# Windowed attention in 64-key blocks on small array tiles, with one score phase and one exp per unit

## The chip, the cores and the metric

The kernel runs on one core of a Trainium2 chip. The core has a matrix engine (PE, whose weight loads are shown apart as PEld), a vector engine (DVE), an activation engine (ACT), a general engine (POOL) and a queue engine for transfers (SP), which run side by side and wait for one another through semaphores. The metric is the time of the kernel on the device in microseconds (us), lower being better.

## The reference

Two branches share a layer norm `xn` of the input (2048 tokens, 512 features, bf16). The attention branch computes, with 32 heads of 16 features,

```python
off = jnp.arange(8) * 2                       # the token itself and 7 more, two apart
idx = pos[:, None] - off[None, :];  mask = idx >= 0
logits = einsum("bhsd,bhswd->bhsw", q, k[idx]) * 16 ** -0.5     # -1e9 where not mask
s = (einsum("bhsw,bhswd->bhsd", softmax(logits), v[idx])) @ wo
```

The other branch is a mixer with an MLP: `x1 = xn + shifted(gelu(LN(xn) @ w1)) @ w2`, then `x1 + gelu(LN(x1) @ w3) @ w4` with 1376 hidden features. The output is `x + s * silu(other branch)`.

Because the offsets are two apart, a token only meets tokens of its own parity: in each parity's own order, of 1024 tokens, a query attends to itself and the 7 tokens ahead of it.

## The kernel before

The tokens are held by parity (p = 0, 1). The first half of the kernel makes the projections: transposed q and k (lines 317 to 323), the shifted mixer (329 to 362), the first MLP matmul w3 (392 to 399). The transposed k and q are kept twice (e = 0, 1 for even and odd heads), so that a group of 32 partitions holds 16 features of one head and 16 rows of a mask; the mask rows come from a table in DRAM through `fill_mask` (lines 218 to 227), and their product pushes a score outside of the window far below zero. So a score matmul has 32 rows, and exp needs no mask of its own. The mask rows repeat with a period of 15 groups of 8 tokens, that is 120.

Attention then runs in **units** (lines 52 to 57): a unit has up to 128 keys of one parity and the 120 queries whose windows lie in them; the first unit has 128 queries with 128 keys, the last 56 with 64. With 9 units for each parity there are 18, taken in order by the loop at line 652. In each iteration n:

- `scores(p, u, 0)`: 16 matmuls of 32 rows by 128 columns (line 461), four row tiles of the array at a time, into two PSUM tiles `s` and `t` of two banks each; for each of them one exp on ACT (line 468) of 128 x 960, which writes the unnormalised weights `prob`.
- first fill: part of a `w4` tile (line 413, 11 matmuls a tile; the second MLP matmul; line 420 to 423 then apply its residual and the silu by DVE, ACT, DVE), scalings, an output tile.
- `scores(p, u, 1)`: the other 16 matmuls and two exps, into the same PSUM tiles.
- second fill: the rest of the `w4` tile.
- `weighted` of the unit before (line 489): 32 matmuls of 128 rows by 32 columns, four column tiles at a time; the stationary operand is `v_aug`, 16 columns of values and 16 of the constant 2, so that each head also yields its denominator. One DVE cast (line 496) gathers the result in `orw`.
- `values` of the next unit (line 440): 4 dense matmuls, and a DVE cast to `v_aug` (line 445).
- last fill: loads and stores.

All these matmuls are pinned (`pin`): they run in the order written. The other instructions are ordered by a planner.

Each parity's units form three **runs** (line 61: units 0 to 2, 3 to 5, 6 to 8), with two `orw` buffers in all. At the end of a run `normalise` sends the denominators through DRAM to a dense layout (SP, lines 511 and 517) and the numerators to `oT` by eight POOL DMAs (line 521). Two units later `normalise_mid` takes the reciprocals on DVE (line 533) and spreads them by SP DMAs (534, 539); four units later `normalise_end` scales `oT` (line 545). Then `final_tile` (line 573) can multiply 128 tokens by `wo`, and DVE and POOL or DVE finish them (582, 584).

Eight PSUM banks are shared out at line 616: two for `s`, two for `t`, two for `o`, one for `w` (w4 tiles), one for `b` (values and `wo`). Tiles 0 to 7 of `w4` go to units 0 to 7, tiles 8 to 11 to the rest; parity 0's eight output tiles go to units 10 to 17. Behind the loop (lines 666 to 686, the **tail**) come w4 tiles 12 to 15, the last scalings and parity 1's eight output tiles.

## Time and profile before

| | us |
|---|---|
| times of three runs | 224.55, 227.35, 228.18 (median 227.35) |
| span of the profiled execution | 222.8 (its time is not given beside it) |
| first stage to the first complete score phase | 0 to 114.1 |
| attention loop, 18 units | 114.1 to 199.3 |
| tail | 199.3 to 222.8 |
| DVE casts of the weighted sum, line 496 | 19.7 for 18 |
| exp on ACT, line 468 | 62.7 for 72 |

A span is counted from the first to the last instruction of the program; the time has some start and end around it. "PE busy" counts the modelled length of pipelined matmuls, so it says that PE has work and not that it is at its peak. Small matmuls on different tiles of the array overlap; what such a phase costs is read from the starts of the phases, not from the sum of the instructions. In a view by stage, the granted clock of PE is given as a share of full speed: it is 0.70 between 114.08 and 119.71, and 1.00 in the rest of the loop.

### The profile page before, as it was taken

To read this page: it belongs to the slowest core of one execution; us is meant where nothing else is said; L and a number is where in the kernel's file an instruction comes from. 1 tells how busy PE (TensorE), PEld (TensorE's weight loads), DVE (VectorE), ACT (ScalarE), POOL (GpSimd) and SP (SyncE) were. 2 spreads that over 40 slices of the span, in tenths; PEclk is the share of its full clock that TensorE was granted. 3 is DMA by queue.
4 is the path that set the end of the run, shared out by engine and by line. 5 is a ranking of instruction groups with operands and counts; after the bars stand their busy time and mean duration, and the time that the engine had idled before them with its cause. 6 is when DMAs were issued, how large, how long until landed. Compare 5 with 4: busy or idle time off the path is not lost.

```text
span 222.8 us, 4851 instructions
## 1 busy us (share of the span) xinstructions
PE 205.6 (92%) x1992; PEld 95.3 (43%) x1992; DVE 130.1 (58%) x244; ACT 136.2 (61%) x158; POOL 61.9 (28%) x119
## 2 busy tenths in 40 slices
PE   8799999999999999999869999999969999999961
PEld 2335545444444444444323444444434445454420
DVE  6689964127279683000103566678457857795984
ACT  2086696956913615665457888898776978842110
POOL 1723563502002202000000007015074482947040
PEclk9999999999999999999988999999999999999998
DMA  5999100130390675799995005526650342625222
GB/s 160 371 392 388 47 0 4 4 8 0 122 161 3 171 195 154 170 118 121 119 122 60 0 3 119 157 68 159 209 125 13 101 83 70 154 51 148 67 85 94
DMA packets 32957, 25.60 MB, mean 115 GB/s; under 512 B 16152, under 2 KB 28792, under 8 KB 32936
## 3 DMA queue, kind: packets, MB, share of 16 engines
q1 hardware_dynamic: 30312, 22.16, 42.7%
q0 software_dynamic: 1536, 2.10, 4.9%
q10 hardware_dynamic: 1088, 1.05, 1.3%
q8 instruction: 15, 0.25, 0.5%
q14 instruction: 6, 0.05, 0.1%
HBM read 16.58 MB, written 4.52 MB: 95 GB/s over the span
## 4 chain that ended last, share of the span: by engine, by line
PE 67%; DMA 10%; DVE 8%; ACT 7%; POOL 2%; SPq 2%; issue 2%; DVEq 0%; ACTq 0%
PE w_ps L413 17%; PE qk_ps L317 9%; PE w_ps L392 9%; ACT prob L468 6%; PE w_ps L329 6%; PE w_ps L357 6%; PE s_ps L461 5%; PE v_ps L440 5%; PE wo_ps L573 4%; DMA qT_159<-mask_d 4%; DMA kT_155<-mask_d 4%; PE o_ps L489 3%; DVE l1s L253 2%; SPq L224 2%; DMA oT_1494<-orw 2%
## 5 line engine op out<-in xcount | busy, mean ns | idle before, releaser
L468 ACT ACTIVATE prob<-s_ps 128x960 bf16<-128x960 f32 (+2 forms) x72 | 62.7, 925 | 15.1 <-PE s_ps L461 14.1
L413 PE MATMUL w_ps<-w_sb,h3T 128*128 128x512 bf16 (+1 forms) x176 | 44.9, 390 | 0.0
L392 PE MATMUL w_ps<-x1nT,w_sb 128*128 128x512 bf16 (+1 forms) x176 | 38.3, 379 | 0.0
L397 ACT ACTIVATE h3T<-w_ps 128x1024 bf16<-128x1024 f32 x20 | 20.5, 1024 | 25.6 <-PE w_ps L392 23.3
L521 POOL DMA_DIRECT2D oT_1494<-orw x24 | 12.4, 523 | 68.2 <-DVE orw L496 68.2
L392 PEld LDWEIGHTS <-w_sb 128*128 128x128 bf16 (+1 forms) x176 | 17.6, 100 | 20.4
L413 PEld LDWEIGHTS <-h3T 128*128 128x128 bf16 (+1 forms) x176 | 15.1, 99 | 17.3 <-issue 1.0
L496 DVE CAST orw<-o_ps 128x960 bf16<-128x960 f32 (+2 forms) x18 | 19.7, 1098 | 1.3 <-PE o_ps L489 1.1
L445 DVE CAST v_aug_148<-v_ps 128x512 bf16<-128x512 f32 (+1 forms) x9 | 6.1, 682 | 23.0 <-PE v_ps L440 23.0
L317 PEld LDWEIGHTS <-wqk_sb 128*128 128x128 bf16 x128 | 12.1, 98 | 12.9
L317 PE MATMUL qk_ps<-xnT_152,wqk_sb 128*128 128x512 bf16 x64 | 15.3, 379 | 0.8 <-DVE xnT_152 L291 0.8
L420 DVE TENSOR_TENSOR xn_95<-w_ps,xn_95 128x512 bf16<-128x512 f32 x8 | 5.5, 684 | 16.5 <-PE w_ps L413 16.5
L329 PE MATMUL w_ps<-xn2T,w_sb 128*128 128x512 bf16 x64 | 14.6, 379 | 0.0
L317 PE MATMUL qk_ps<-xnT_153,wqk_sb 128*128 128x512 bf16 x64 | 14.5, 379 | 0.0
L584 POOL TENSOR_TENSOR xo_1715<-sg,xo_1715 128x512 bf16<-128x512 bf16 x8 | 10.4, 1297 | 14.5 <-DVE sg L582 13.4
L362 DVE TENSOR_TENSOR xn_95<-w_ps,xn_95 128x1024 bf16<-128x1024 f32 x4 | 4.9, 1215 | 14.4 <-PE w_ps L357 14.4
L422 ACT ACTIVATE sig<-xn_96 128x512 bf16<-128x512 bf16 x8 | 5.0, 630 | 12.6 <-DVE xn_96 L420 12.6
L521 POOL DMA_DIRECT2D oT_2418<-orw x24 | 12.1, 513 | 1.6 <-DVE orw L496 1.6
L246 POOL TENSOR_SCALAR l3r<-l3m 128x4 f32<-128x4 f32 x4 | 0.9, 232 | 36.7 <-DVE l3m L254 36.7
L440 PE MATMUL v_ps<-wv_sb,xnT_153 128*128 128x512 bf16 (+1 forms) x36 | 9.3, 380 | 2.0 <-DVE sg L582 2.0
L461 PE MATMUL s_ps<-qT_159,kT_155 32*128 32x120 bf16 (+2 forms) x144 | 7.7, 214 | 3.1 <-DMA qT_159<-mask_d 3.1
L573 PE MATMUL wo_ps<-wo_sb,oT_2418 128*128 128x512 bf16 x32 | 7.6, 379 | 2.2 <-DVE oT_2418 L545 2.2
(132 smaller groups left out, 329.3 us busy)
## 6 DMA issues: line engine op xcount, KB each, us to landing
w_sb<-in_B_w_dram SPq DMA_DIRECT2D x1, 1376.0 KB, 9.5
w_sb<-in_B_w_dram SPq DMA_DIRECT2D x1, 1280.0 KB
wqk_sb<-in_A_wqkv_dram SPq DMA_DIRECT2D x2, 512.0 KB
w_sb<-in_B_w_dram SPq DMA_DIRECT2D x2, 512.0 KB, 6.0
xn_96<-in_A_x_dram SPq DMA_DIRECT2D x4, 256.0 KB, 6.9
xo_1715<-in_A_x_dram SPq DMA_DIRECT2D x4, 256.0 KB, 5.5
xo_2325<-in_A_x_dram SPq DMA_DIRECT2D x4, 256.0 KB, 4.5
out_dram<-xo_1715 SPq DMA_DIRECT2D x4, 256.0 KB, 3.8
```

The costliest lines, as they stand in the source:

```text
L317: nc.tensor.matmul(pt[:, b, :], lhsT=wqk_sb[:, dt, nt * P : (nt + 1) * P], rhs=xnT[p][:, dt, cs], start=(dt == 0), stop=(dt == ND - 1),)
L329: nc.tensor.matmul(pt[:, b, :], lhsT=w1_sb[:, dt, g * P : (g + 1) * P], rhs=xn2T[:, dt, :], start=(dt == 0), stop=(dt == ND - 1),)
L357: nc.tensor.matmul(pt[:, j, :], lhsT=w2_src(p, g, m0), rhs=w2_sb[:, g, :], start=(g == 0), stop=(g == ND - 1),)
L392: nc.tensor.matmul(pt[:fs, ft % 2, :], lhsT=w3_sb[:, dt, ft * P : ft * P + fs], rhs=x1nT[:, dt, :], start=(dt == 0), stop=(dt == ND - 1),)
L397: last["gelu"] = nc.scalar.activation(h3T[:, 2 * a : 2 * a + 2, :], pt, AF.Gelu_apprx_tanh)
L413: nc.tensor.matmul(pt, lhsT=h3[c][:fs, ft, jj * P : (jj + 1) * P], rhs=w4_sb[:fs, ft, :], start=(ft == 0), stop=(ft == NF - 1),)
L440: nc.tensor.matmul(vp[:nk, :], lhsT=xnT[p][:, dt, k0 : k0 + nk], rhs=wv_sb[:, dt, :], start=(dt == 0), stop=(dt == ND - 1),)
L461: nc.tensor.matmul(st[:nk, b, i * nq : (i + 1) * nq], lhsT=kT[p][e][r : r + 32, dt, k0 : k0 + nk], rhs=qT[p][e][r : r + 32, dt, q0 : q0 + ...
L468: nc.scalar.activation(prv[:nk, 2 * h : 2 * h + 2], st[:nk, :, 0 : 4 * nq], AF.Exp, scale=SCALE)
L496: nc.vector.tensor_copy(out=orw[p][:, :, :, q0 - ra : q0 - ra + nq], in_=op[:, :, 0 : 4 * nq].rearrange("p j (s q) -> p j s q", q=nq),)
L521: nc.gpsimd.dma_start(out=oT[p][DH * hh : DH * (hh + 1), :, ra : ra + rw], in_=orw[p][32 * cg : 32 * cg + DH, jj],)
L573: nc.tensor.matmul(pt[:, j, :], lhsT=oT[p][:, dt, (i + j) * P : (i + j + 1) * P], rhs=wo["sb"][:, dt, :], start=(dt == 0), stop=(dt == ND ...
```

## The change

Keys are taken in blocks of 64 in place of 128. A unit has still 128 keys, two blocks s = 0, 1 on the lower and upper half of the partitions, and block s meets 64 queries alone: keys k0 to k0+63 meet queries k0+8 to k0+71, keys k0+64 to k0+127 meet queries k0+64 to k0+127. The 8 queries k0+64 to k0+71 are met by both blocks, and their two partial sums, numerators and denominators, are added. So a unit yields 120 queries again, and units start at k0 = 56 + 120 u, eight for each parity. The first 64 tokens of both parities, with the first 64 keys each, form one joint unit (`None`), in the loop between the parities: 17 units.

- `scores` is one phase: 64 matmuls of 32 rows by 64 columns with 64 queries each, on tiles at (32 r, 64 s), into one PSUM tile `s` of four banks, and one exp of 128 x 2048.
- `weighted` has 64 matmuls of 64 rows by 32 columns, on tiles at (64 s, 32 cg), with 64 queries each. DVE casts the 2 x 56 queries that only one block meets, copies the 8 shared ones of the second block to a small tile, and adds those of the first.
- In an iteration all fill work comes last: scores, weighted of the unit before, values of the next one, then the w4 part, scalings, output tile, loads and stores.
- Runs are units 0 to 2, 3 to 5, 6 to 7, and the joint unit is a run `first` of its own for both parities (16 POOL DMAs, two scalings), with its gathered result in a buffer of the `s4` group.
- Output tiles 1 to 7 of parity 0 go to units 10 to 16; tile 0 goes to the tail, and so does `normalise_mid` of parity 1's second run. The tail uses the four banks of `s` singly (f, g, h, i).
- The mask table is read 8 columns further on, to fit the new start of the units.

Lines that are taken out of `values`, `scores` and `weighted` are left out here; they stand above.

```diff
@@ -45,24 +45,20 @@
     NCH = S // CH
     TPC = CH // P
     M = S // 2
-    NQ = 120
     PEN = 512.0
-
-
-    units = [(0, P, 0, P)]
-    while units[-1][0] + units[-1][1] < M:
-        q0 = units[-1][0] + units[-1][1]
-        nq = min(NQ, M - q0)
-        units.append((q0, nq, q0 - W, nq + W))
+    KB = P // 2
+    QU = P - W
+
+
+    units = [KB - W + u * QU for u in range((M - KB) // QU)]
     NU = len(units)
 
 
     runs = []
-    for cuts in ((0, 3, 6, NU), (0, 3, 6, NU)):
-        runs.append(
-            [(a, b, units[a][0], sum(units[u][1] for u in range(a, b))) for a, b in zip(cuts[:-1], cuts[1:])]
-        )
-    RW = max(r[3] for rs in runs for r in rs)
+    for a, b in ((0, 3), (3, 6), (6, NU)):
+        q0 = units[a] + W
+        runs.append((a, b, q0, units[b - 1] + P - q0))
+    RW = max(r[3] for r in runs)
...
         nc.vector.tensor_tensor(
-            out=tab[:, :, 0:P], in0=tab[:, :, 0:P], in1=ident.unsqueeze(1).to_broadcast([P, 3, P]), op=ALU.mult
+            out=tab, in0=tab, in1=ident.unsqueeze(1).to_broadcast([P, 3, P]), op=ALU.mult
         )
         g = small.tile([P, 4], F32, name="mg", tag="mg", bufs=1)
-        nc.vector.tensor_reduce(out=g[:, 0:3], in_=tab[:, :, 0:P], axis=mybir.AxisListType.X, op=ALU.add)
...
     def values(p, u):
         va = v_aug[cnt["v"] % NV]
         cnt["v"] += 1
         vp = pst("b", "v_ps")[:, 0, :]
         for dt in range(ND):
+            first, last_ = dt == 0, dt == ND - 1
+            if p is None:
+                for s in range(2):
                     pin(
                         nc.tensor.matmul(
+                            vp[KB * s : KB * s + KB, :], lhsT=xnT[s][:, dt, 0:KB], rhs=wv_sb[:, dt, :],
+                            start=first, stop=last_, tile_position=(0, KB * s),
                         )
                     )
+            else:
+                k0 = units[u]
+                pin(
+                    nc.tensor.matmul(
+                        vp, lhsT=xnT[p][:, dt, k0 : k0 + P], rhs=wv_sb[:, dt, :], start=first, stop=last_
+                    )
                 )
+        nc.vector.tensor_copy(out=va[:, :, 0:DH], in_=vp.rearrange("p (h d) -> p h d", d=DH))
+        return va
+
+    def scores(p, u):
+
+        pr = sm4.tile([P, 4, 2 * ND, KB], BF16, name="prob", tag="s4")
+        st = pst("s", "s_ps").rearrange("p r (i q) -> p r i q", q=KB)
+        for i in range(2 * ND):
+            dt, e = i // 2, i % 2
+            for s in range(2):
+                pp, k0 = (s, 0) if p is None else (p, units[u] + KB * s)
+                q0 = k0 if p is None or s else k0 + W
+                for r in range(4):
+                    rows = slice(32 * r, 32 * r + 32)
                     pin(
                         nc.tensor.matmul(
+                            st[KB * s : KB * s + KB, r, i, :], lhsT=kT[pp][e][rows, dt, k0 : k0 + KB],
+                            rhs=qT[pp][e][rows, dt, q0 : q0 + KB], start=True, stop=True,
+                            tile_position=(32 * r, KB * s),
                         )
                     )
+        with tc.issue_after(last["gelu"].ins):
+            nc.scalar.activation(pr, st, AF.Exp, scale=SCALE)
+        return pr
+
+    def weighted(p, u, va, pr):
+
+        if p is None:
+            key, rw = "first", P
+        else:
+            r = next(i for i, x in enumerate(runs) if u < x[1])
+            key, (a, b, ra, rw) = (p, r), runs[r]
+        if p is None or u == a:
+            if p is None:
+                t = sm4.tile([P, 2 * ND * rw], BF16, name="orw0", tag="s4")
+            else:
+                t = orwp.tile([P, 2 * ND * RW], BF16, name="orw", tag="orw")[:, 0 : 2 * ND * rw]
+            orw[p] = t.rearrange("p (g q) -> p g q", g=2 * ND)
+        op = pst("o", "o_ps")
+        for g in range(2 * ND):
+            jj, dt = g // ND, g % ND
+            for s in range(2):
+                for cg in range(4):
+                    h = 4 * jj + cg
+                    pin(
+                        nc.tensor.matmul(
+                            op[32 * cg : 32 * cg + 32, s, g * KB : (g + 1) * KB],
+                            lhsT=va[KB * s : KB * s + KB, dt * 8 + h, :],
+                            rhs=pr[KB * s : KB * s + KB, h // 2, 2 * dt + h % 2, :],
+                            start=True, stop=True, tile_position=(KB * s, 32 * cg),
+                        )
+                    )
+        ow = orw[p]
+        ov_ = op.rearrange("p s (g q) -> p s g q", q=KB)
+        if p is None:
+            nc.vector.tensor_copy(out=ow.rearrange("p g (s q) -> p s g q", s=2), in_=ov_)
+            normalise(key, rw, [(0, 0, KB), (1, 0, KB)])
+        else:
+            c, n = units[u] + W - ra, KB - W
+            wide = lambda t, off, step, width: bass.AP(
+                t.tensor, t.offset + off, [list(t.ap[0]), [step, 2], list(t.ap[-2]), [1, width]]
+            )
+            nc.vector.tensor_copy(out=wide(ow, c, KB, n), in_=wide(ov_, 0, CH + W, n))
+            mix = small.tile([P, 2 * ND, W], F32, name="mix", tag="mix")
+            nc.vector.tensor_copy(out=mix, in_=ov_[:, 1, :, 0:W])
+            nc.vector.tensor_tensor(out=ow[:, :, c + n : c + KB], in0=ov_[:, 0, :, n:KB], in1=mix, op=ALU.add)
+            if u == b - 1:
+                normalise(key, rw, [(p, ra, rw)])
...
+        c = 0
+        for p, q0, nq in parts:
+            for jj in range(2):
+                for cg in range(4):
+                    hh = 4 * jj + cg
+                    nc.gpsimd.dma_start(
+                        out=oT[p][DH * hh : DH * (hh + 1), :, q0 : q0 + nq],
+                        in_=w[32 * cg : 32 * cg + DH, ND * jj : ND * jj + ND, c : c + nq],
+                    )
+            c += nq
+        rrs[key] = (dn, rden_d, w, rw, parts)
+
+    def normalise_mid(key):
+        dn, rden_d, w, rw, parts = rrs[key]
         n = H * rw // P
         rb = small.tile([P, n], BF16, name="rb", tag="rb", bufs=1)
...
@@ -613,76 +633,72 @@
     stage_w3(2)
     stage_w3(3)
 
-    layout(s=2, t=2, o=2, w=1, b=1)
+    layout(s=4, o=2, w=1, b=1)
     NW = 12
     w4s = [w4_tile(t // TPC, t % TPC, t >= NW) for t in range(S // P)]
 
-    fill = {n: ([], [], []) for n in range(2 * NU)}
-
-    for n in range(2 * NU):
-        t, a, b, c = (
-            (n, 0, 9, NF) if n < 8
-            else ((8, 0, 3, 4), (8, 4, 9, NF), (9, 0, 4, 4), (9, 4, 8, 8), (9, 8, NF, NF), (10, 0, 4, 4),
-                  (10, 4, 8, 8), (10, 8, NF, NF), (11, 0, 5, 6), (11, 6, NF, NF))[n - 8]
-        )
-        fill[n][0].append(lambda t=t, a=a, b=b: w4s[t](a, b))
+
+    order = [(0, u) for u in range(NU)] + [(None, 0)] + [(1, u) for u in range(NU)]
+    NN = len(order)
+    fill = [[] for _ in range(NN)]
+    split = (
+        [(8, 0, 6)], [(8, 6, NF)], [(9, 0, 4)], [(9, 4, 8)], [(9, 8, NF)], [(10, 0, 4)], [(10, 4, 8)],
+        [(10, 8, NF), (11, 0, 3)], [(11, 3, NF)],
+    )
+    for n in range(NN):
+        for t, a, b in [(n, 0, NF)] if n < 8 else split[n - 8]:
+            fill[n].append(lambda t=t, a=a, b=b: w4s[t](a, b))
         if n >= 10:
-            fill[n][0].append(lambda i=n - 10: final_tile(0, i, 1, nc.gpsimd))
-        if n >= 12 and n % 2 == 0:
-            fill[n][2].append(lambda i=n - 12: store(nc.sync, 0, i))
-        if c > b:
-            fill[n][1].append(lambda t=t, b=b, c=c: w4s[t](b, c))
-
-    for p in range(2):
-        for r, (_, end, _, _) in enumerate(runs[p]):
-            n = p * NU + end
-            if n + 2 < 2 * NU:
-                fill[n + 2][0].insert(0, lambda p=p, r=r: normalise_mid(p, r))
-            if n + 4 < 2 * NU:
-                fill[n + 4][0].insert(0, lambda p=p, r=r: normalise_end(p, r))
+            fill[n].append(lambda i=n - 9: final_tile(0, i, 1, nc.gpsimd))
+        if n in (12, 14, 16):
+            fill[n].append(lambda i=n - 10: store(nc.sync, 0, i))
+
+    ends = [((0, 0), 3), ((0, 1), 6), ((0, 2), 8), ("first", 9), ((1, 0), 12), ((1, 1), 15)]
+    for key, n in ends:
+        if n + 2 < NN:
+            fill[n + 2].insert(0, lambda key=key: normalise_mid(key))
+        if n + 4 < NN:
+            fill[n + 4].insert(0, lambda key=key: normalise_end(key))
     for w in range(2):
-        fill[w][2].append(lambda w=w: fill_mask(1, w))
-    fill[8][2].append(load_wo)
+        fill[w].append(lambda w=w: fill_mask(1, w))
+    fill[9].append(load_wo)
     for k in range(4):
-        fill[5 + k][2].append(lambda k=k: load_xo(0, k))
-        fill[11 + k][2].append(lambda k=k: load_xo(1, k))
-    order = [(p, u) for p in range(2) for u in range(NU)]
+        fill[5 + k].append(lambda k=k: load_xo(0, k))
+        fill[11 + k].append(lambda k=k: load_xo(1, k))
     va = values(*order[0])
     prev = None
     for n, (p, u) in enumerate(order):
-        prs = [scores(p, u, 0)]
-        for f in fill[n][0]:
-            f()
-        prs.append(scores(p, u, 1))
-        for f in fill[n][1]:
-            f()
+        pr = scores(p, u)
         if prev is not None:
             weighted(*prev)
-        prev = (p, u, va, prs)
-        if n + 1 < len(order):
+        prev = (p, u, va, pr)
+        if n + 1 < NN:
             va = values(*order[n + 1])
-        for f in fill[n][2]:
+        for f in fill[n]:
             f()
-    weighted(*prev, tag="s")
+    weighted(*prev)
+    layout(f=1, g=1, h=1, i=1, o=2, w=1, b=1)
     w4s[NW](0, NF)
+    normalise_mid((1, 1))
     w4s[NW + 1](0, NF)
-    store(nc.sync, 0, 6)
-    normalise_mid(1, 2)
-    normalise_end(1, 1)
-    final_tile(1, 0, tag="t")
+    normalise_mid((1, 2))
+    final_tile(0, 0, tag="f")
+    store(nc.sync, 0, 0)
+    final_tile(1, 0, tag="g")
     w4s[NW + 2](0, NF)
-    final_tile(1, 1, tag="o")
+    normalise_end((1, 1))
+    final_tile(1, 1, tag="h")
     store(nc.scalar, 1, 0)
-    final_tile(1, 2, tag="s")
+    final_tile(1, 2, tag="i")
     w4s[NW + 3](0, NF)
-    normalise_end(1, 2)
-    final_tile(1, 3, eng=nc.gpsimd, tag="t")
+    normalise_end((1, 2))
+    final_tile(1, 3, eng=nc.gpsimd, tag="f")
     store(nc.scalar, 1, 2)
-    final_tile(1, 4, eng=nc.gpsimd, tag="o")
-    final_tile(1, 5, tag="s")
+    final_tile(1, 4, eng=nc.gpsimd, tag="g")
+    final_tile(1, 5, tag="h")
     store(nc.scalar, 1, 4)
-    final_tile(1, 6, tag="t")
-    final_tile(1, 7, tag="o")
+    final_tile(1, 6, tag="i")
+    final_tile(1, 7, tag="f")
     store(nc.scalar, 1, 6)
 
 

```

## The prediction

> **What bounds the kernel now.** I read the busy shares, then busy time by stage, then the chain of waits inside one unit of attention.
>
> ```profile
> PE 205.6 (92%) x1992; PEld 95.3 (43%) x1992; DVE 130.1 (58%) x244; ACT 136.2 (61%) x158; POOL 61.9 (28%) x119
> ```
>
> PE is busy 92% of the span, but a busy PE is not a PE at its peak, so the stages decide. The next view gives, for each stretch in us: its length, then busy time (and instructions) of PE, weight loads, DVE, ACT and POOL, the granted clock, the DMA share and GB/s.
>
> ```profile
> 114.08:119.71 5.63, 5.62 (x36) 2.08 (x36) 0.69 (x1) 2.99 (x4) 0.00 (x0) 0.70 1.06 119
> 119.71:153.71 34.00, 33.95 (x555) 15.40 (x554) 22.55 (x30) 29.63 (x37) 8.33 (x16) 1.00 0.28 68
> 153.71:157.20 3.49, 3.39 (x74) 1.67 (x74) 3.12 (x5) 2.34 (x5) 0.00 (x0) 1.00 0.79 242
> 157.20:199.30 42.10, 38.62 (x714) 19.08 (x714) 29.55 (x41) 33.45 (x40) 21.89 (x32) 1.00 0.38 96
> 199.30:222.83 23.53, 16.69 (x76) 7.18 (x76) 16.69 (x27) 2.52 (x4) 7.25 (x11) 0.96 0.33 100
> ```
>
> Attention lasts from 114.08 (the last mask transfer lands) to 199.30: 85.2 us for 18 units; the tail takes 23.5. In the first half PE has no hole and ACT is busy 29.63 of 34.00. One unit there, from the chain (start, length, what):
>
> ```profile
> 124.99 0.34 PE s_ps L461 x16
> 125.33 2.05 PE w_ps L413 x9
> 127.38 0.34 PE s_ps L461 x16
> 127.72 0.54 PE w_ps L413 x2
> 128.26 0.53 PE o_ps L489 x32
> 128.80 0.97 PE v_ps L440 x4
> ```
>
> All six phases are PE: 4.77 us. Nine dense matmuls take 2.05 and two 0.54, so one is (2.05-0.54)/7 = 0.2157 and each phase loses 0.54-0.43 = 0.11 on top: a gap at each change of tile shape, six per unit. In the second half the chain alternates between engines:
>
> ```profile
> 181.65 0.39 PE s_ps L461 x8
> 182.03 0.97 PE w_ps L413 x4
> 183.00 0.86 PE wo_ps L573 x4
> 183.86 0.43 PE s_ps L461 x16
> 184.29 1.83 ACT prob L468 x2
> ```
>
> Here the exps hold up the scores, which need their PSUM back: two exps on the path, then eight matmuls, then PE again.
>
> **The change, part by part.** Durations by shape:
>
> ```profile
> L468 ACT ACTIVATE prob<-s_ps 128x960 bf16<-128x960 f32 x56 | 51.2, 967 | 10.5 <-PE s_ps L461 9.6 <-issue 0.7
> L496 DVE CAST orw<-o_ps 128x960 bf16<-128x960 f32 x14 | 16.1, 1151 | 1.3 <-PE o_ps L489 1.1
> L496 DVE CAST orw<-o_ps 128x448 bf16<-128x448 f32 x2 | 1.2, 612 | 0.0
> 160.55 0.39 PE L489 MATMUL o_ps<-prob,v_aug_148 64*32 64x56 bf16 x32
> 160.87 1.04 PE L440 MATMUL v_ps<-wv_sb,xnT_153 128*128 128x512 bf16 x4
> ```
>
> *Exp.* Four instructions of 960 columns per unit become one of 2048. Two of 960 in a row take 1.83 and two of 1024 take 1.94 (at 113.58): 0.86 ns a column, so 2048 columns take 0.97+1024*0.00086 = 1.85 us in place of 3.66. On the first half's path this is worth nothing (PE is the chain); in the second it removes the alternation. The score banks are now one buffer of four, so the next scores wait for the exp; PE has the weighted phase, values and w4 or wo in between, at least 2.4 us against 1.85 plus some 0.15 of handover. Without that cover each unit would lose the difference.
>
> *Matmuls of scores and weighted sum.* 32+32 per unit become 64+64, of 64 columns, on eight tiles at a time. Today 32 weighted ones of 120 columns take 0.53-0.11 = 0.42, eight rounds of four, 52 ns a round; with 56 columns the two timeline rows above leave 160.87-160.55-0.11 = 0.21, 26 ns a round: 0.41 ns a column, so 64 columns make 29 ns. The 32x64 scores of the short unit (56 columns) stand at 153.71 to 153.97 for 16: (0.26-0.11)/4 = 37 ns a round at most, and their starts late in it lie 30 ns apart. No row has eight tiles at work. Lower end: eight run as four do, 8 rounds each: scores 8*0.031 = 0.25, weighted 8*0.029 = 0.235. Upper end: still four at a time, 16 rounds: 0.50 (0.60 at 37 ns) and 0.47. Within a group of four, starts lie about 3.5 ns apart, and 8*3.5 = 28 ns just fits into a round; so I take the lower end plus a tenth: 0.28 and 0.26.
>
> A page of the Trainium skill speaks against this: "TensorE: Matmul & The Clock Gate", section "Wait — 56ns, not 53.3ns?", says that starts never lie closer than about 25 ns however small the matmul is. By it 128 matmuls would take 3.2 us a unit and the kernel would be far slower (an estimate from that page); the row above has 32 of them start in 0.21 us, so the floor, if it is one, holds per tile.
>
> *Gaps.* Scores, weighted, then values and w4 (and wo) in one dense stretch: three gaps of 0.11, not six.
>
> *DVE.* One cast of 960 becomes a cast of 896, a copy of 64 and an add of 64 that waits for it. Slope (1151-612)/512 = 1.05 ns: 1.08, 0.21, 0.21. Instructions in a row overlap by some 0.08 (176.09 to 177.16 for 1.15), so about 1.4 us against 1.07. The copy and add are in no row: between 0.17 (the smallest 128-partition DVE rows, 2 columns) and 0.61 (448 columns) each; I take the straight line.
>
> *Buffers of the gathered output.* There are two, and the fill work now comes behind the weighted phase. So in units 7, 10 and 16 the first cast of a run wants the buffer that the scaling issued in the same unit gives back. The scaling (0.9) then runs ahead of the cast; behind the cast stand only the next weighted phase, a unit later, and the values' cast. At most 0.9 three times, part of the waits below; it grows if the broadcast of the reciprocals, issued two units earlier, has not landed.
>
> *First tokens.* One joint unit replaces two units of 128 queries, and the 56-query units go: 17 units for 18. Its 16 POOL DMA issues of 0.51 are 8.2 us of a POOL queue busy 21.89 of 42.10; its user comes four units later, so I count nothing; uncovered, they delay the adds of the first output tiles, not PE. The extra mean and broadcast DMAs on SP likewise have two units each.
>
> **The sum**, against the profiled execution (span 222.8).
> - Unit 0: one score phase and its gap less, the same half clock: 5.63 to 5.4.
> - Units 1 to 7: 15*0.2157 + 0.28 + 0.26 + 0.33 = 4.11; 28.8 against 34.0.
> - Units 8 to 16 against 153.71 to 199.30 (45.6). PE: 9*0.87 = 7.8; values 8*0.863 = 6.9; w4 tiles 8 to 11, 44*0.2157 = 9.5; seven wo tiles 6.0; the last weighted phase 0.4: 30.6. DVE: output copies 12.4, 23 ops of 512 columns at 0.60 = 13.8, reciprocals and scalings 4.9: 31.1. The two are level and pass one bank ("b": values, its cast, wo, its multiply, values) between them, so I add 5 us of waits, where the old stretch had 3.6: 35.6.
> - Tail: output tile (0,0) comes in (0.86 of PE, 0.69+0.42 of DVE), a reciprocal and a scaling too; but only two tiles, not three, now wait for the last scaling. +1.0.
>
> -0.2-5.2-10.0+1.0 = -14.4: span 208.4. The page gives the span alone; the three times lie 1.8, 4.6 and 5.4 above it. With the median's 4.6 I forecast 213.0.
>
> The skill's "TensorEngine Tiling (Array Packing)", section "PSUM Bottleneck", warns that tiling doesn't speed up emptying PSUM. The DVE sum above agrees for the second half: by the rule alone that half could not go below 31.1; by PE's rows, below 30.6.
>
> **Rivals.**
> 1. *Four tiles at a time.* (0.50-0.28)+(0.47-0.26) = 0.43 a unit, times 17 = 7.3, of which the waits of the second half take up 1 or 2: about 219. For it: no row shows row and column tiles together. Against it: rows alone and columns alone each overlap fully.
> 2. *DVE becomes the bound of the second half.* If the 896-column cast, which now spans two banks, or the small pair costs 0.9 more, nine units lose 8: about 221. For: DVE is level with PE already. Against: today's cast also takes two banks in one instruction.
> 3. *Slower: the supply of PE's instructions.* 128 loads and matmuls in a row come in each unit; before has no such run longer than 32 pairs (6.5 ns each). Assumed: 0.54/128 = 4.2 ns a pair. There are 17*128 = 2176 pairs, so 14.4 us are gone at 4.2+6.6 = 10.8 ns a pair, and from there it is slower; at 14 ns it would be +7, about 234.
> 4. *No gain to speak of:* waits of 2 and rounds of 1 together, about 225.
>
> **Chances.** Forecast 0.57 (207.5 to 217); rival 1 0.15; rival 2 0.13; rival 3 0.10; rival 4 0.05. Three times of the kernel before spread over 1.6%, so 2% is about what can be told from no change: faster is below 222.8. Faster 0.57+0.15+0.10 = 0.82, within 2% 0.03+0.05 = 0.08, slower 0.10. The range leaves out rivals 3 and 4 and a little at each end: 207.5 to 222.5.
>
> **What would show it.** In a first-half unit: 64 scores in about 0.39 with their gap, 64 weighted in 0.37, starts of eight within one round of 31 ns; a period near 4.1; no wait of PE on the exp, whose row shows 17 of 1.85. In the second half: PE idle by some 5 us, on the casts of values or on the wo multiply. Attention's end near 184 and a tail of 24.5. Wrong if the score phase lasts 0.6 or more, if the period of the second half lies above 4.5, or if PE waits on its own queue inside the small matmuls.

## The result

The changed kernel is slower. Its median is 243.8 us (241.9 to 244.7; 244.2 with a fourth run of 246.0) against 226.6 for the kernel before: ratio 1.081, 95% interval 1.072 to 1.090. Medians of changed kernels, here and below, leave out runs more than 1.5% above the fastest of the same kernel, as the ratios do. The profiled execution of the changed kernel took 244.65 us with a span of 242.9, where the forecast had a span of 208.4.

First the page of the changed kernel, its row for PE.

```profile
PE 206.7 (85%) x2987; PEld 100.3 (41%) x3016; DVE 135.0 (56%) x278; ACT 105.6 (43%) x103; POOL 67.8 (28%) x134
```

ACT is relieved, as meant (136 to 106 us), but PE is no less busy, with half as many instructions again. Next, busy time by stage with the columns as before: length, PE, weight loads, DVE, ACT, POOL, granted clock, DMA share, GB/s. The joint unit's scores begin at 155.23, the tail at 211.80.

```profile
114.31:120.59 6.28, 6.06 (x68) 2.52 (x69) 0.69 (x1) 3.16 (x2) 0.00 (x0) 0.58 0.99 111
120.59:155.23 34.64, 32.40 (x1000) 18.01 (x1007) 23.88 (x42) 16.76 (x14) 8.33 (x16) 1.00 0.28 69
155.23:169.15 13.92, 11.23 (x409) 6.17 (x411) 8.45 (x16) 6.67 (x5) 9.12 (x19) 0.88 0.48 133
169.15:185.41 16.26, 7.55 (x145) 3.22 (x146) 5.51 (x11) 1.88 (x1) 4.12 (x7) 0.69 0.19 55
185.41:211.80 26.39, 21.11 (x761) 11.96 (x765) 20.40 (x36) 11.16 (x8) 15.37 (x22) 1.00 0.34 80
211.80:242.90 31.10, 21.13 (x78) 8.39 (x80) 18.30 (x31) 2.52 (x4) 6.33 (x10) 0.77 0.25 76
```

| stage | before | forecast | changed kernel | off the forecast |
|---|---|---|---|---|
| start of the first complete score phase | 114.1 | 114.1 | 114.3 | +0.2 |
| unit 0 | 5.63 | 5.4 | 6.28 | +0.9 |
| units 1 to 7 | 34.0 | 28.8 | 34.64 | +5.8 |
| units 8 to 16 | 45.6 | 35.6 | 56.57 | +21.0 |
| tail | 23.5 | 24.5 | 31.10 | +6.6 |

The last column adds up to the 34.5 us between the spans. No stage gained. In the third and fourth rows PE has nothing to do for 11.4 of 30.2 us, and in the first, third, fourth and last the granted clock is below full.

One first-half unit from the chain of the changed kernel (start, length, what):

```profile
131.47 0.64 PE s_ps L466 x64
132.10 0.61 PE o_ps L496 x64
132.72 0.32 PE v_ps L447
...
133.69 2.38 PE w_ps L410 x11
136.06 0.73 PE s_ps L466 x64
```

It takes 4.59 us where 4.11 was forecast. Scores take 0.64 in place of 0.39 and the weighted sums 0.61 in place of 0.37: those two make up the whole difference. The starts in the trace say how: in each phase 32 pairs of load and matmul run as forecast, eight tiles in 32 ns (32 pairs in 0.14 us), then comes a hole of 0.07 to 0.10 us, and the other 32 start 8.3 ns apart (0.26 us).

The casts and the exp came as forecast (1.85; 1.08, 0.21, 0.21), in the groups by form:

```profile
L473 ACT ACTIVATE prob<-s_ps 128x2048 bf16<-128x2048 f32 x17 | 31.7, 1866 | 23.4 <-PE s_ps L466 23.4
L513 DVE CAST orw<-o_ps 128x896 bf16<-128x896 f32 x16 | 17.4, 1088 | 4.3 <-PE o_ps L496 4.1
L516 DVE TENSOR_TENSOR orw<-o_ps,mix 128x64 bf16<-128x64 f32 x16 | 3.5, 217 | 0.1
L515 DVE COPY mix<-o_ps 128x64 f32<-128x64 f32 x16 | 3.4, 215 | 0.0
```

The longest single wait is PE's for the output weights, 7.7 us to 176.89. SP's queue just before it (start, length, what):

```profile
164.87 0.52 SPq L529 DMA_DIRECT2D den_d<-orw  x1
169.48 0.32 SPq L535 DMA_DIRECT2D dn<-den_d  x1
169.85 0.42 SPq L554 DMA_DIRECT2D rden_d<-rb  x1
171.64 0.62 SPq L559 DMA_DIRECT2D orw<-rden_d  x1
172.31 0.45 SPq L576 DMA_DIRECT2D wo_sb<-in_A_wo_dram  x1
```

The joint unit's divisors go out at 164.87, but reading them back (`dn`, 169.48) waits, since the one `dn` buffer still holds run (0,2)'s divisors until their reciprocal at 168.95. Behind it stand two transfers that need that reciprocal, and behind those `wo_sb` (the output weights), which in the kernel before was issued at 154.31.

In the timeline of PE, the end of the loop and the tail show further waits (start, length, what, in brackets the idle time before it and what ended it):

```profile
211.07 0.71 PE L496 MATMUL o_ps<-prob,v_aug 64*32 64x64 bf16 x64 [3.00 <-DVE orw L516]
213.40 0.61 PE L410 MATMUL w_ps<-w_sb,h3T 128*128 128x512 bf16 x1 [1.62 <-DVE orw L516]
214.23 6.66 PE L410 MATMUL w_ps<-w_sb,h3T 128*128 128x512 bf16 x20 [0.22 <-issue]
...
229.99 2.76 PE L593 MATMUL wo_ps<-wo_sb,oT 128*128 128x512 bf16 x12 [0.89 <-DVE oT L568]
234.99 2.94 PE L593 MATMUL wo_ps<-wo_sb,oT 128*128 128x512 bf16 x8 [2.23 <-DVE oT L568]
```

Twenty w4 matmuls take 6.66 us instead of the 4.3 that they take at full clock: the trace has the granted clock at half from 211.80 to 218.63, behind the idle time. The 3.00 has its cause in the chain before it:

```profile
202.10 3.33 POOL oT L541 x7
205.43 0.18 issue
205.62 3.61 DMA oT<-orw
...
209.44 1.09 DVE orw L513
...
211.07 0.77 PE o_ps L496 x64
```

The first cast of run (1,2) wants an `orw` buffer, and gets the one whose numerators POOL has only just begun to send off: eight issues and a landing lie between.

### The profile page after: what moved, and what is told of

Read it like the earlier page. It is cut to its first block, busy times and chain, and to the rows that moved or that the text cites. A ratio compares the mean times of both kernels' runs of the same rounds, so it can differ in the third digit from the quotient of the medians.

```text
span 242.9 us, 6871 instructions
## 1 busy us (share of the span) xinstructions
PE 206.7 (85%) x2987; PEld 100.3 (41%) x3016; DVE 135.0 (56%) x278; ACT 105.6 (43%) x103; POOL 67.8 (28%) x134
## 4 chain that ended last, share of the span: by engine, by line
PE 51%; DMA 19%; DVE 14%; POOL 6%; issue 5%; SPq 2%; ACT 1%; DVEq 0%; ACTq 0%
PE w_ps L410 9%; PE qk_ps L314 9%; PE w_ps L389 8%; PE w_ps L354 6%; PE w_ps L326 6%; POOL oT L541 4%; DVE orw L513 4%; DMA kT<-mask_d 4%; DMA oT<-orw 4%; DMA qT<-mask_d 4%; PE v_ps L447 3%; PE wo_ps L593 3%; PE o_ps L496 3%; PE s_ps L466 3%; DMA rden_d<-rb 2%
## 5 line engine op out<-in xcount | busy, mean ns | idle before, releaser
L541 POOL DMA_DIRECT2D oT<-orw x64 | 32.5, 516 | 72.4 <-PE w_ps L410 50.3
L473 ACT ACTIVATE prob<-s_ps 128x2048 bf16<-128x2048 f32 x17 | 31.7, 1866 | 23.4 <-PE s_ps L466 23.4
L314 PE MATMUL qk_ps<-xnT,wqk_sb 128*128 128x512 bf16 x125 | 29.6, 379 | 1.0 <-DVE xnT L288 0.8
L593 PE MATMUL wo_ps<-wo_sb,oT 128*128 128x512 bf16 x64 | 17.5, 414 | 11.7 <-DMA wo_sb<-in_A_wo_dram 7.7
L604 POOL TENSOR_TENSOR xo<-sg,xo 128x512 bf16<-128x512 bf16 x9 | 10.8, 1195 | 35.2 <-ACT sig L419 15.0
L447 PE MATMUL v_ps<-wv_sb,xnT 128*128 128x512 bf16 x49 | 17.3, 415 | 3.2 <-issue 2.5
L513 DVE CAST orw<-o_ps 128x896 bf16<-128x896 f32 x16 | 17.4, 1088 | 4.3 <-PE o_ps L496 4.1
L320 ACT ACTIVATE qT<-qk_ps 128x1024 bf16<-128x1024 f32 x16 | 15.2, 1031 | 6.0 <-PE qk_ps L314 5.9
L496 PE MATMUL o_ps<-prob,v_aug 64*32 64x64 bf16 x1088 | 12.4, 199 | 5.7 <-DVE orw L516 3.5
L420 DVE SCALAR_TENSOR_TENSOR xn<-sig,xn 128x512 bf16<-128x512 bf16 x16 | 12.0, 752 | 8.3 <-ACT sig L419 8.3
L466 PE MATMUL s_ps<-qT,kT 32*64 32x64 bf16 x1088 | 13.3, 209 | 3.7 <-DMA qT<-mask_d 3.3
```

The costliest lines, as they stand in the source:

```text
L314: nc.tensor.matmul(pt[:, b, :], lhsT=wqk_sb[:, dt, nt * P : (nt + 1) * P], rhs=xnT[p][:, dt, cs], start=(dt == 0), stop=(dt == ND - 1),)
L320: nc.scalar.activation(dst[e][:, n0 : n0 + 2, cs], pt, AF.Copy)
L447: nc.tensor.matmul(vp, lhsT=xnT[p][:, dt, k0 : k0 + P], rhs=wv_sb[:, dt, :], start=first, stop=last_)
L466: nc.tensor.matmul(st[KB * s : KB * s + KB, r, i, :], lhsT=kT[pp][e][rows, dt, k0 : k0 + KB], rhs=qT[pp][e][rows, dt, q0 : q0 + KB], start ...
L473: nc.scalar.activation(pr, st, AF.Exp, scale=SCALE)
L496: nc.tensor.matmul(op[32 * cg : 32 * cg + 32, s, g * KB : (g + 1) * KB], lhsT=va[KB * s : KB * s + KB, dt * 8 + h, :], rhs=pr[KB * s : KB ...
```

## The experiments

Two theories stood against each other. **Q**: the loss is the order of the queues and the buffers around the joint unit and the scalings. **I**: it is the supply of PE's instructions for the small matmuls. A third, **F**, came up with the holes inside the small matmuls: there PE waits for a fetch of its instructions that stands behind other transfers. Two narrower ones follow Q: **J**, the joint unit's work in the queues holds `wo_sb` back; **L**, the new division of the banks makes the first matmul of the tail wait.

The kernel before was run again beside each set of runs, with medians of 225.4 to 226.9 us. Times of different sets are therefore comparable to about 1.5 us; the ratios are free of this.

**Output weights one step earlier.**

```diff
-    fill[9].append(load_wo)
+    fill[8].append(load_wo)
```

> The changed kernel with one line moved: the load of the output weights (wo_sb) is issued one step earlier (list 8 instead of 9), ahead of the divisor work of run (0,2) in SP's queue. Theory Q (a queue's order is the largest loss): the 7.7 us in which TensorE waits for wo_sb are gone, and part of the half-speed stretch that follows an idle TensorE with them; 244.2 becomes 233 to 237 us. Theory I (instruction supply and the small matmuls are the loss; the wait for wo_sb only stands in for another that is late a moment later, the normalised outputs that the same matmul reads): TensorE waits on for the scaling of (0,2), and the time falls by under 3 us, to 241 or more.

236.3 us, ratio 1.045 (1.034 to 1.055). The wait for `wo_sb` is gone, 7.5 us are won. Theory Q holds for this wait.

**Two buffers for divisors and reciprocals.**

```diff
-        dn = small.tile([P, n], BF16, name="dn", tag="dn", bufs=1)
+        dn = small.tile([P, n], BF16, name="dn", tag="dn", bufs=2)
-        rb = small.tile([P, n], BF16, name="rb", tag="rb", bufs=1)
+        rb = small.tile([P, n], BF16, name="rb", tag="rb", bufs=2)
```

> The changed kernel with two buffers instead of one for the divisors (dn) and for their reciprocals (rb). In the loop the load of dn for the joint unit no longer waits for the reciprocal of run (0,2), but wo_sb still stands behind the two transfers of (0,2) that wait for that reciprocal: the 7.7 us stay within 1 us. In the tail the divisors of run (1,2) no longer wait for the reciprocal of (1,1). Theory Q: the end comes 2 to 5 us earlier, 239 to 242 us. Theory I: the tail is as long as its matmuls at the clock that they get, and the time stays within 1 us of 244.

240.6 us, 1.065 (1.055 to 1.075): 3.2 us won with the wait for `wo_sb` still 7.3 us long, as theory Q has it.

**Scalings ahead of the weighted sums.** `normalise_mid` and `normalise_end` move from `fill[n]` to a list that is called between scores and weighted sums.

```diff
+        for f in pre[n]:
+            f()
         if prev is not None:
             weighted(*prev)
```

> The changed kernel with the reciprocals and the scalings of finished runs written ahead of a unit's weighted sums instead of behind them: in VectorE's queue they then stand ahead of the casts of that unit. Theory Q: the buffer orw is given back before the next run's first cast asks for it, and the waits of the weighted phases before the bank comes free (0.5 at 153.5, about 1 at 170, 3.0 and 1.6 at 208 to 213) go: 5 to 6 us in sum, 238 to 240 us, unless the scaling itself still waits for the numerators' transfers, in which case VectorE waits at another place of its queue and 1 to 3 us are won. Theory I: no change beyond 1 us.

240.5 us, 1.063 (1.050 to 1.076). The wait of 3.0 us is gone, that before the tail is 2.2 in place of 1.6; 3.3 us are won of the 5 to 6. The intervals of this run and of the one before it just overlap that of the changed kernel, so the size of these two gains is rough.

**The three together.**

> The three edits together: output weights earlier, two buffers for divisors and reciprocals, scalings ahead of the weighted sums. Theory Q: 244.2 less 8 to 11, less 2 to 5, less 1 to 6: about 228, between 222 and 233 us; that is the time of the kernel before, and what then remains against the forecast of 213 is the instruction supply (about 7.5 us of slow second halves of the score and weighted phases and about 4.7 us of holes with fetches). Theory I: 240 or more.

235.9 us, 1.040 (1.030 to 1.049): both theories miss. The edits don't add up (7.5+3.2+3.3 apart, 7.9 together). In its trace PE now waits for VectorE up to 173.5 (2.0 us), holes with no releaser remain at 122 (2.0) and 161.7 (2.4), with a half-clock stretch behind the latter, and the tail still starts with a wait of 2.2.

**A ground for the rest.** In the runs that follow, the four chunks `x1nT` are read back as they lie: the transposition is left out, and the layers behind it compute on other numbers in the same sizes.

```diff
-        pin(nc.sync.dma_start_transpose(out=x1nT, in_=x1n_dram[c * CH : (c + 1) * CH, :]))
+        pin(
+            nc.sync.dma_start(
+                out=x1nT, in_=x1n_dram[c * CH : (c + 1) * CH, :].rearrange("(i q) d -> q i d", q=P)
+            )
+        )
```

> The changed kernel, but the four chunks that are read back transposed ahead of the third layer of the network (x1nT) are read back as they lie: the transposition is left out, and the layers behind it compute on other numbers in the same sizes. It is the ground for the runs that follow, which have the same edit. The loads lie between 60 and 91 us of the span, ahead of the attention. Both theories: within 1.5 us of 244, and the same waits from the first score phase on.

241.7 us, 1.064 (1.059 to 1.070), 2.1 us less than the changed kernel (a little more than the 1.5 allowed for), with the same waits (7.77 for `wo_sb`, 2.87 and 1.62 at the end of the loop). This is what the next runs are compared with. The kernel before was not run in this form, so a ratio from here on flatters the change by some 2 us.

**The score phase in two halves.**

```diff
+            if i == ND:
+                between()
...
+        pr = scores(p, u, lambda: n < 8 and w4s[n](0, 4))
```

> On the ground of plain loads (the transposition of x1nT left out). In units 0 to 7 the first four of the eleven matmuls of the last layer of the network stand between the two halves of the score phase (32 pairs, then the other 32), the other seven behind the weighted sums and ahead of the values. Theory I (the instructions are handed to TensorE at about 8.3 ns a pair once some 32 pairs that lay ready are used up): after the four large matmuls the second half runs like the first, 32 pairs in about 0.14 us instead of 0.26, with no hole of 0.1 us ahead of it; the weighted phase, left as it is, keeps its slow second half. The time hardly moves, since two more changes between large and small matmuls cost 0.1 to 0.2 us each: within 3 us of the ground. Rival (the second half is slow by itself, by its operands or its place in the banks): 0.26 us again, wherever it stands.

240.0 us, 1.059 (1.050 to 1.067). The time can't be told from the ground's. In the timeline of PE:

```profile
126.47 0.33 PE L472 MATMUL s_ps<-qT,kT 32*64 32x64 bf16 x32
126.73 1.04 PE L414 MATMUL w_ps<-w_sb,h3T 128*128 128x512 bf16 x4
127.69 0.33 PE L472 MATMUL s_ps<-qT,kT 32*64 32x64 bf16 x32
127.95 0.73 PE L502 MATMUL o_ps<-prob,v_aug 64*32 64x64 bf16 x64
```

Both halves of the scores are over in 0.26 us, change of shape included, and their starts span 0.139 us each. The weighted phase now follows directly upon a half that has used up what lay ready, and all its pairs but the first five start 8.3 ns apart, without the quick first half that it has elsewhere. So neither operands nor banks make a half slow: after some 64 instructions the rest arrive at one in 4.2 ns. The unit takes 4.63 us against 4.59, since each change of shape costs its own gap; splitting is no remedy.

**Mask transfers two units later.**

```diff
-        fill[w].append(lambda w=w: fill_mask(1, w))
+        fill[w + 2].append(lambda w=w: fill_mask(1, w))
```

> On the ground of plain loads. The mask transfers of parity 1 are issued in units 2 and 3 instead of 0 and 1. Theory F (the hole of 1.5 to 2.6 us in the weighted phase of unit 0, which all runs so far show at 121 to 124 us, is a fetch of instructions that stands behind those transfers): the hole is gone or under 0.5 us there, and one may come up two units later instead; 1 to 3 us off the ground. Rival (the hole comes with the place in the instruction stream, whatever the transfers do): it stays at the same matmul, with 1.5 us or more, and the time stays.

245.1 us, 1.080 (1.074 to 1.085): 3 us slower than the ground, where a gain was expected. The hole in the weighted phase of unit 0 is gone, but a longer one comes with the transfers. They slid behind a wait in SP's queue, and its timeline has the last eight at

```profile
131.85 8.62 SPq L221 DMA_DIRECT2D qT<-mask_d  x8
```

while PE's has

```profile
139.38 0.54 PE L470 MATMUL s_ps<-qT,kT 32*64 32x64 bf16 x44
143.38 0.38 PE L470 MATMUL s_ps<-qT,kT 32*64 32x64 bf16 x20 [3.46 <-issue]
```

with the DMA engines busy throughout and one 16 KB packet of the instruction queue among them. From 142.6 to 149.4 the clock is halved.

**No mask transfers for parity 1.**

```diff
-    for w in range(2):
-        fill[w].append(lambda w=w: fill_mask(1, w))
```

> On the ground of plain loads. The sixteen mask transfers of parity 1 (2 MB) are left out, and with them the masking of that parity; all else stays. Theory F (an instruction fetch that meets those transfers leaves TensorE without instructions): the hole of 3.2 us at 118 to 122 us is gone, none of over 1 us comes up in its place in units 0 to 7, the clock that is granted there stays at full speed, and 3 to 6 us are won, 236 to 239. Rival (the place in the instruction stream alone decides): a hole of 1.5 us or more at the same matmul, and the time of the ground.

235.0 us, 1.041 (1.034 to 1.049): 6.7 us under the ground by the times, 5.2 by the ratios, where 3 to 6 were expected. This kernel leaves out the masking of parity 1. The ground's timeline of PE in iteration 1, where unit 0's weighted sums stand, and then the same place here:

```profile
117.20 0.70 PE L470 MATMUL s_ps<-qT,kT 32*64 32x64 bf16 x64
117.83 0.61 PE L500 MATMUL o_ps<-prob,v_aug 64*32 64x64 bf16 x55
121.64 0.23 PE L500 MATMUL o_ps<-prob,v_aug 64*32 64x64 bf16 x9 [3.20 <-issue]
121.80 1.28 PE L451 MATMUL v_ps<-wv_sb,xnT 128*128 128x512 bf16 x4
122.88 4.03 PE L414 MATMUL w_ps<-w_sb,h3T 128*128 128x512 bf16 x11
```

```profile
115.83 0.71 PE L470 MATMUL s_ps<-qT,kT 32*64 32x64 bf16 x64
116.47 0.68 PE L500 MATMUL o_ps<-prob,v_aug 64*32 64x64 bf16 x64
117.08 1.04 PE L451 MATMUL v_ps<-wv_sb,xnT 128*128 128x512 bf16 x3
117.96 2.54 PE L414 MATMUL w_ps<-w_sb,h3T 128*128 128x512 bf16 x11
```

From one score phase to the next it is 9.63 us in the first and 4.60 in the second. The hole is 3.20 of the 5.0, the half clock behind it (eleven w4 matmuls in 4.03, not 2.54) most of the rest. This shows that the transfers make the hole: same instructions, same place, no transfers, no hole. That it is a fetch of instructions, as theory F has it, is read from the instruction queue, which the trace shows as queue q8. From the ground's DMA view between 117 and 121.7 us:

```profile
q8 instruction: 1, 0.02, 2.3%
```

This packet of 16 KB lies at 118.62 to 120.34, and PE goes on at 121.64, 1.30 us behind its end. The traces of all kernels here bear this out: from 112 us on they have 56 waits of PE of over 0.25 us without a releaser, and each ends 0.96 to 1.89 us behind the end of such a packet, 54 of them 1.25 to 1.63 behind it. The trace of the changed kernel has 23 such packets, that of before 15, and before has no such wait. The transfers alone do not set the length of the hole: in two other runs that issue the same ones, that with the scores split and that with the joint unit earlier (below), there is none over 0.25 us at this place, and one of 0.51.

**Queue edits, later masks and a reordered tail.** The tail's edit, beside those already shown:

```diff
-        if n >= 10:
+        if 10 <= n < 16:
             fill[n].append(lambda i=n - 9: final_tile(0, i, 1, nc.gpsimd))
...
-    w4s[NW](0, NF)
     normalise_mid((1, 1))
-    w4s[NW + 1](0, NF)
+    w4s[NW](0, NF)
     normalise_mid((1, 2))
+    w4s[NW + 1](0, NF)
     final_tile(0, 0, tag="f")
     store(nc.sync, 0, 0)
+    final_tile(0, 7, tag="h")
+    store(nc.sync, 0, 6)
```

> On the ground of plain loads. The three edits of the first runs (output weights earlier, two buffers for divisors and reciprocals, scalings ahead of the weighted sums), the mask transfers two units later, and the tail in another order: the reciprocals of the last two runs stand ahead of the first two tiles of the tail in VectorE's queue, and the last output tile of the loop behind the last weighted sums. Theory Q: 8 us off the ground for the three edits, 1.5 for the mask, 2 to 4 for the tail: 230 to 233 us if the ground is 244. Theory I: 235 or more, as the matmuls of the tail set its length.

Inconclusive: 235.0 us over all four runs, which lie between 229.2 and 237.7, and no ratio. In its profile PE stands twice in the middle of the loop: 3.46 us from 140.3 without a releaser, beside the moved masks, and 4.37 us from 154.6, waiting for VectorE.

**Joint unit two units earlier.**

```diff
-    order = [(0, u) for u in range(NU)] + [(None, 0)] + [(1, u) for u in range(NU)]
+    order = [(0, u) for u in range(6)] + [(None, 0)] + [(0, u) for u in range(6, NU)] + [(1, u) for u in range(NU)]
...
-    ends = [((0, 0), 3), ((0, 1), 6), ((0, 2), 8), ("first", 9), ((1, 0), 12), ((1, 1), 15)]
+    ends = [((0, 0), 3), ((0, 1), 6), ("first", 7), ((0, 2), 9), ((1, 0), 12), ((1, 1), 15)]
```

> On the ground of plain loads. The joint unit stands two units earlier, between units 5 and 6 of parity 0 instead of behind unit 7, so that its divisors (dn) and its sixteen transfers on GpSimd's queue no longer fall in with those of run (0,2). Theory J (the joint unit's work in the queues, which the forecast counted at nothing, is what holds wo_sb back): the load of dn for the run behind it waits for a reciprocal that is already done, wo_sb is issued in its own step, the 7.8 us wait is gone: 7 to 10 us off the ground, 232 to 235. Rival (any run that ends two units ahead of wo_sb holds it): the wait stays above 4 us.

234.0 us, 1.038 (1.024 to 1.051): 7.7 us off the ground by the times, 6.1 by the ratios, and PE no longer waits for `wo_sb`, which SP issues at 151.14. Theory J holds: with the joint unit away from run (0,2), `wo_sb` goes out in time from its old place.

**Joint unit, queue edits and tail together, with the scalings first and last.** `joint_p`'s order, earlier weights, two buffers, the tail as above; the second run has the scalings back behind the weighted sums.

> On the ground of plain loads. Joint unit two units earlier, output weights one step earlier, two buffers for divisors and reciprocals, scalings ahead of the weighted sums, the reordered tail; masks as in the changed kernel. Theory Q: 241.7 less 7 to 10 for the wait, less 3 to 5 for the scalings and the tail: 227 to 232 us, the time of the kernel before; the slow halves of the phases (7.6 us) and the holes with fetches remain, and they are why it is not 213. Theory I: 235.

> As the run before it, with the scalings back behind the weighted sums. They hold the casts of the first unit of a run back there by 3.0 and 1.6 us, ahead of them by about 2 at one place: 0 to 3 us longer than the run before it.

228.7 us, 1.014 (1.007 to 1.022), and 237.9 us, 1.051 (1.040 to 1.062). The first lies within the 227 to 232 of theory Q. The scalings' place alone is worth 9 us here, three times what was expected: with them last, weighted phases wait 3.46, 2.46 and 3.94 us, the first of them for a scaling that stands in VectorE's queue ahead of the cast and waits itself for POOL's transfer of numerators.

**Banks of the tail**, kept as in the loop, on the ground and on the 228.7 us run.

```diff
-    layout(f=1, g=1, h=1, i=1, o=2, w=1, b=1)
+    tail4 = pst("s", "wo_ps")
...
-        pt = pst(tag, "wo_ps")
+        pt = pst(tag, "wo_ps") if tag == "b" else tail4[:, "fghi".index(tag) : "fghi".index(tag) + 1, :]
```

> On the ground of plain loads (241.7 us), one edit: the tail keeps the division of the banks of the loop, and its output tiles take the four banks of one score tile. Theory L (the new division makes the first matmul of the tail wait until every cast of the last weighted sums is done): the wait of 1.6 us before that matmul is under 0.3 and the half-speed stretch of 3.4 us behind it is gone or shorter; 1.5 to 3 us off the ground. Rival (VectorE is late whatever the banks, or the tail is bound by its reciprocals): the same wait, or the won time is lost again before the last output tiles; within 1 us of the ground.

> The run with the joint unit earlier and the queue edits (228.8 us), and the banks of the loop kept in the tail. Theory L: the wait of 2.6 us goes and with it 1.7 us of the half-speed stretch at 203.0 to 206.4: 224 to 227 us. Rival: 228 or more.

242.5 us, 1.078 (1.064 to 1.092), and 231.5 us, 1.033 (1.020 to 1.046): the first matmul of the tail no longer waits, yet nothing is won. (The second is if anything slower; its interval and that of the 228.7 us run overlap.) PE's timeline of the first:

```profile
205.99 0.74 PE L500 MATMUL o_ps<-prob,v_aug 64*32 64x64 bf16 x64 [3.36 <-DVE orw L520]
206.66 0.61 PE L414 MATMUL w_ps<-w_sb,h3T 128*128 128x512 bf16 x1
207.49 6.59 PE L414 MATMUL w_ps<-w_sb,h3T 128*128 128x512 bf16 x20 [0.22 <-issue]
```

The bank wait is gone, but the slow stretch is as long as before (half clock from 204.93 to 211.75), so the wait for the `orw` buffer ahead of it is enough to bring it. (With the scalings first, where only the wait of 2.2 before the tail is left, the trace has the clock at full there.) And of the second:

```profile
203.82 1.03 PE L597 MATMUL wo_ps<-wo_sb,oT 128*128 128x512 bf16 x4
205.69 1.02 PE L597 MATMUL wo_ps<-wo_sb,oT 128*128 128x512 bf16 x4 [0.85 <-DVE sg L606]
```

Output tiles in one tile of four banks wait for one another, and from 220.05 to the end the clock is at half.

**Mask transfers thinned out**, on the 228.7 us run, alone and with the banks kept.

```diff
-    def fill_mask(p, w):
+    def fill_mask(p, w, ks=range(8)):
...
-    for w in range(2):
-        fill[w].append(lambda w=w: fill_mask(1, w))
+    for n, w, ks in [(0, 0, (0, 1, 2)), (1, 0, (3, 4, 5)), (2, 0, (6, 7)), (2, 1, (0,)), (3, 1, (1, 2, 3)), (4, 1, (4, 5, 6, 7))]:
+        fill[n].append(lambda w=w, ks=ks: fill_mask(1, w, ks))
```

> The run with the joint unit earlier and the queue edits (228.8 us), and the sixteen mask transfers of parity 1 two to four to a unit over units 0 to 4 instead of eight to a unit in units 0 and 1. Theory F: the hole of 1.2 us in the weighted phase of unit 0 goes, none of over 1 us comes in units 0 to 6; 1 to 3 us off. Rival (SP hands the sixteen on in one go anyway, since it runs ahead of the matmuls): the hole moves or stays, and the time is the same.

> Both edits on top of the run with the joint unit earlier: 222 to 225 us by theories L and F together, 1 to 2% below the kernel before; by their rivals 228. What is then left against 213 is 7.6 us of slow halves (17 units, two phases, 0.22 us each), the holes of units 7 to 10 and VectorE's waits in the second half.

233.9 us, 1.045 (1.032 to 1.059), and 236.6 us, 1.058 (1.048 to 1.067): misses. The hole of unit 0 is gone, but the last seven transfers slid behind a wait in SP's queue to 132.9, and the joint unit's scores wait for them.

**The new banks behind the first two tiles of the tail**, on the 228.7 us run; in the second run the residual loads come later too.

```diff
-    layout(f=1, g=1, h=1, i=1, o=2, w=1, b=1)
     normalise_mid((1, 1))
     w4s[NW](0, NF)
     normalise_mid((1, 2))
     w4s[NW + 1](0, NF)
+    layout(f=1, g=1, h=1, i=1, o=2, w=1, b=1)
```

> The run with the joint unit earlier and the queue edits (228.8 us, plain loads), and the new division of the banks placed behind the first two tiles of the tail. Theory L: no wait before the first matmul of the tail (2.6 us before), at most a small one before the first output tile; with the half-speed stretch behind the wait gone too: 224 to 226.5 us. Rival (what is won there is lost before the last output tiles, which wait for the reciprocals of the last run): 227.5 or more.

> The run before it, and the residual loads of parity 0 issued three units later, those of parity 1 one unit later. Theory F: the hole of 3.5 us at 159 to 162.5 us (a fetch of instructions beside two residual loads and the output weights) is under 1.5 us: 2 to 3 us below the run before it. Rival (other transfers take their place beside the next fetch): a hole of 2 us or more within units 6 to 10, and the same time.

227.9 us, 1.008 (1.003 to 1.013; ten runs), and 228.2 us, 1.012 (0.995 to 1.029). In the first, PE's timeline runs through the start of the tail at full clock:

```profile
200.24 4.93 PE L414 MATMUL w_ps<-w_sb,h3T 128*128 128x512 bf16 x22
205.00 2.75 PE L597 MATMUL wo_ps<-wo_sb,oT 128*128 128x512 bf16 x12
```

Against the 1.014 before it the gain in time isn't told from none. A hole of 1.47 was left there at 160.4; in the second run it is 2.36, so later loads are no cure. No version here beats the kernel before: the best has 1.008, with plain loads that save some 2 us by themselves.

## Why the prediction was wrong

By its steps:

- *Exp* and *DVE*: the exp right to 1%, the DVE instructions to 4%, and PE never waited on an exp. Moving them off the path gained nothing, since PE took more.
- *Matmuls of scores and weighted sum*: the rounds were right (eight tiles in 32 ns), but only half of them ran so. "The lower end plus a tenth", 0.54 a unit, holds for 32 pairs of each phase; the other 32 are held to 8.3 ns. Measured without the gaps: 0.53+0.50 = 1.03, that is 8.0 ns a pair. Rival 3 named this, with its point of decision at 10.8 ns; at 8.0 it costs 17*0.49 = 8.3 us and leaves a gain. By itself it would have given 221, inside the range. The Trainium skill's "TensorE: Matmul & The Clock Gate", section "The mechanism", speaks of a window of 64 instructions in which loads are pulled ahead; the 32 quick pairs are 64 instructions, which agrees. That the window is what sets their number, no run here shows.
- *First tokens*, "I count nothing" and "two units each": this is the step that failed most. Its queue work was put at nothing and cost 7.7 us. The joint unit's divisors met run (0,2)'s in the one `dn` buffer, SP's queue stood still behind them, and `wo_sb` with it, shown by the runs with the joint unit or the weights earlier. The forecast followed POOL's queue and the users of its transfers, and not what SP holds back when one of its own entries waits.
- *Buffers of the gathered output*, "at most 0.9 three times": 3.00 for one of them in the changed kernel, up to 3.94 in the 237.9 us run, since the buffer that is given out is not the one that the scaling frees but the one that POOL is still emptying (4.0 us of issues, 3.6 to land).
- *The 5 us of waits* of the second half, taken from the old stretch: PE's waits for VectorE come to 0.50+0.33+0.37+1.06+3.00 = 5.3, but that is luck, since 3.00 of it is the buffer of the gathered output; and there was no term for holes. The changed kernel's profile has holes with no releaser of 1.47, 0.40 and 0.75 us inside small phases and one of 2.03 ahead of values. The first goes with the mask transfers. The others end 1.43, 1.49 and 1.38 us behind a packet of the instruction queue, as the first does (1.40), so they look like fetches too; but no run took them away, and what made these fetches late stays open.
- *Tail*, +1.0: +7.6. The wait of 1.62 comes from the new division of the banks, shown by the runs without and with a later one. The half clock behind it and the 3.00 adds 2.3, and without the 1.62 it was there all the same. The one `dn` buffer and the late reciprocal of (1,1) hold the last scaling back; two buffers won 3.2.
- *The clock* was a term only in unit 0. There it was longer than counted: two steps here (half clock from 112.82 to 119.64), one in the kernel before (115.18 to 118.59), hence the +0.9. Most long waits and several holes meet one to three further stretches of 3.41 us at half clock. In units 1 to 7, slow halves 3.4 and holes 1.9 explain 5.3 of the 5.8. In units 8 to 16, slow halves 4.4, `wo_sb` 7.7, holes 2.8 and waits 0.3 over the forecast explain 15.2 of 21.0; the rest I put to the clock (0.69 in the stretch from 169.15), which no run takes away by itself.

The nearest that the sum comes to closing is the 227.9 us run, whose span of 226.1 is 17.7 above the forecast: one hole and its half clock (9.45 for a unit of 4.60) 4.9, slow halves of 16 units 7.8, the tail 25.8 for 24.5. Against that, attention starts 1.2 earlier, and unit 0, at full clock, takes 3.9 for 5.4. The 6.4 that remain lie in the later units, among them the 1.47 hole with its stretch and a wait of 2.4 on VectorE; they are not split further.

The step from span to time was too large as well: 4.6 us were added, the distance from the profiled execution's span to the median, while an execution's time lies 1.7 to 2.8 above its own span in all runs here, mostly 1.8. By this the profiled execution was the fastest of the three. That is small beside the 30.8 us between forecast and result.

## What to carry to other kernels

Halving the tile of a small matmul doubles its instructions: look in the trace for the longest run of small pairs, and price what goes beyond it at the steady rate, not at the rate of the burst. When two pieces of work end near each other, walk down each queue past the new waiting instruction and name what stands behind it, loads for later stages above all. And add to each wait of a few us what a halved clock behind it can cost: here 3.2 us of hole cost 5.0.

## What the runs showed of the hardware

- PE took 64 small instructions (32 pairs of load and matmul) in 0.14 us and then one in 4.2 ns, for the 32x64 and the 64x32 tiles alike.
- Instruction fetches are 16 KB packets on their own queue. The Trainium skill's "Runtime: NRT & Kernel Launch", section "Instruction fetch mechanics", calls crossing such a block mostly hidden. It was hidden here in units 0 to 7 without the mask transfers (no such wait over 0.25 us); beside them PE stood for up to 3.5 us. PE went on 1.25 to 1.63 us behind the end of the packet in 54 of 56 such waits.
- Half-clock stretches lie in steps of 3.41 us: those of the changed kernel are 3.41, 6.83 and 10.24 us long, apart from the last, which the end of the program cuts short. One followed a hole of 2.03 us (from 164.0). A hole of 1.47 us at 121.8 had none, while one of 1.47 us at 160.4 in the 227.9 us run had one (from 162.8): the length alone does not decide.
